# Thresholded attention and a gated mix on one core: a schedule written as a list of operations

## The chip, the cores and the metric

The kernel runs on one core of a Trainium2 chip. A core has five engines that run side by side, each with its own queue of instructions that it takes in order: PE (TensorE, matrix products and transposes), DVE (VectorE), ACT (ScalarE), POOL (GpSimd) and SP (SyncE, which here only issues transfers). An instruction waits at the head of its queue until the semaphores that it names have been reached, and all that stands behind it waits too. The metric is the device time in microseconds, the median of several executions. Before the change it is 833.94 us (three runs, 832.13 to 834.44).

## What is computed

Batch 8, 8 heads, 576 tokens, 64 channels per head. Attention keeps only scores within `tau` of the row's maximum. Its output, with the heads side by side as 512 channels, is `x` of a gated mix.

```python
scores = scale * np.matmul(q, k.transpose(0, 1, 3, 2))
thresh = np.max(scores, axis=-1, keepdims=True) - tau
scores = np.where(scores >= thresh, scores, -1000000000.0)
scores = scores - np.max(scores, axis=-1, keepdims=True)
attn = np.exp(scores)
attn = attn / (np.sum(attn, axis=-1, keepdims=True) + 1e-09)
x = np.matmul(attn, v)            # then (B, S, 512)
...
for k in range(5):                # causal convolution along the tokens
    gate_pre += conv_w[k][None, None, :] * xp[:, k:k + S, :]
gate = 1.0 / (1.0 + np.exp(-gate_pre))
out = gate * (x @ w_val) @ w_out
```

Q, K, V are float32; the weights arrive as float64 words and are converted on the chip.

## The kernel before, in words

Heads go in pairs, one over the other in the 128 partitions: 4 pairs in each of 8 batches, 32 pairs. A pair's queries make 9 tiles: one of the first 64 queries of both heads, and 4 of 128 for each head. A float32 operand of the scores and of the products with the weights is split in a high and a low part (`fp32r`), whose products are added.

For each tile: PE forms the scores in the tile `s` of PSUM, which has two rooms (`scores`, L255; four matmuls, six for the tile of both heads). DVE takes the negated maximum (L272), ACT the exponential (L274) and the threshold (L276), DVE compares, multiplies and sums up in one instruction (L292, `Group.keep`). `Group.divide` then adds 1e-9 to the sums (L301, DVE), takes the reciprocals (L304, DVE) and scales the rows (L307, POOL). `Group.turn` transposes the rows in chunks of 128 keys on PE (L319) into `tp` (two rooms of PSUM), and ACT copies them to `T` (L322).

When the tiles of half a pair's queries have been transposed (320 queries in the first half, 256 in the second), `attend_units` (L354 to L362) forms the attended values in an accumulator (`acc`, two rooms of PSUM): one matmul for the last 64 keys of both heads (L355), then eight, four chunks of keys for two heads (L362), the first head to the lower 64 columns of the array and the second to the upper 64. Each matmul of plain float32 has two records in the trace, so these are 2 and 16. The eight come in two units of four, `attend(0)` and `attend(1)`, at two steps of the loop, and within the first of them transposes may be put.

`conv_units` splits the result in two parts and convolves it: one tap on POOL (L395), four on DVE (L402), tanh on ACT (L410). `mix_units` issues the products of a batch, 192 matmuls (L429) in 16 units of 12 (320 or 256 wide), while the next batch attends. DVE multiplies by the gate (L447), ACT and POOL split the result (L452, L454), ACT takes up the second products (L467), and a transfer writes them out.

Beside all that, `Job` fetches q and k of the next pairs, splits them (L202, L204, L216, L218) and spreads the parts over the partitions with 12 transfers per pair from SP's queue (L198). The weights are converted during the first two batches, in 16 pieces of five DVE steps each (`from_f64`, L98 to L113).

The order of the work is written out by hand: the loop at L637 makes one step per tile, `stages` gives each preparation its step, `plan` and `moves` spread the products over the steps between two attentions, and `turns` holds the transposes back by two steps. On top of that the framework may still move an instruction ahead of others of its engine, since the source doesn't ask for its own order.

Of the kernel before, what the change touches and what calls it, by code (L numbers as in the profile page):

```python
# [19 lines left out]
RUN = (2, 3)  # steps between two attentions, in turn  # L20
# [3 lines left out]
def tile_thresholded_attention_gated_mix(  # L24
# [26 lines left out]
    W = [SL + 2 * P, 2 * P]  # the queries of a pair in two parts  # L51
# [9 lines left out]
    qk = ctx.enter_context(tc.tile_pool(name="qk", bufs=2))  # L61
    att = ctx.enter_context(tc.tile_pool(name="att", bufs=2))
    pt = ctx.enter_context(tc.tile_pool(name="pt", bufs=1))
    mix = ctx.enter_context(tc.tile_pool(name="mix", bufs=1))
    ps_s = ctx.enter_context(tc.tile_pool(name="ps_s", bufs=2, space=bass.MemoryType.PSUM))
    ps_t = ctx.enter_context(tc.tile_pool(name="ps_t", bufs=2, space=bass.MemoryType.PSUM))
    ps_a = ctx.enter_context(tc.tile_pool(name="ps_a", bufs=2, space=bass.MemoryType.PSUM))

# [6 lines left out]
    # a negative tau keeps no score, and all keys weigh the same: as if all scores were 0  # L75
# [8 lines left out]
    bdq = [[const.tile([P, P], F32R, name=f"bdq{i}{j}") for j in range(2)] for i in range(2)]  # L84
# [4 lines left out]
    # ---- float64 words to float32: sign, exponent and the mantissa's top 20 bits come from the  # L89
    # high word (nothing below the normal range), the next 16 from the low word's upper half ----  # L90
    def from_f64(words, a, m, f):
        """The pieces of work for a, and one that adds the low word's share."""
        i32 = lambda t: t.bitcast(I32)
        hi, lo = words[..., 1], words.bitcast(U16)[..., 1]
        least = 2.0**-15 * 1.125  # its bits are those of a high word of 2^-126

        def pieces():
            nc.scalar.square(f, hi.bitcast(F32))  # L98
            nc.vector.tensor_scalar(
                i32(m), hi, 3, 0x3FFFFFFF, op0=ALU.logical_shift_left, op1=ALU.bitwise_and  # L100
            )
            yield
            nc.vector.scalar_tensor_tensor(
                i32(a), hi, -(1 << 30), i32(m), op0=ALU.bitwise_and, op1=ALU.bitwise_or
            )
            yield
            nc.vector.scalar_tensor_tensor(
                a, f.bitcast(F32), least * least, a, op0=ALU.is_ge, op1=ALU.mult)
            yield
            nc.vector.tensor_scalar(i32(m), i32(a), -(1 << 23), None, op0=ALU.bitwise_and)  # L110
            yield
            nc.vector.scalar_tensor_tensor(f, lo, 2.0**-36, m, op0=ALU.mult, op1=ALU.mult)
            nc.gpsimd.tensor_add(a, a, f.bitcast(F32))  # L113
            yield

        return pieces()
# [5 lines left out]
    def fetch_conv():  # L122
        nc.sync.dma_start(
            cw_raw.rearrange("p (c k) t -> p c (k t)", c=NE),
            conv_w.bitcast(I32).rearrange("(c p) k -> p c k", p=P),
        )

    CW = DM // 2
    parts = [
        (name, w, c, d0)  # L130
        for name, w in (("wv", w_val), ("wo", w_out))
        for d0 in range(0, DM, CW)
        for c in range(NE)
    ]
    rooms = []
    spare = [const.tile([P, CW], F32, name=f"spare{i}") for i in range(3)]

    def fetch_mix():
        """The words of the next CW columns of 128 rows."""
        if len(rooms) < len(parts):  # L140
            _, w, c, d0 = parts[len(rooms)]
            room = mix.tile([P, S], F32, name="o", bufs=2)
            words = room[:, 0 : 2 * CW].bitcast(I32)
            nc.sync.dma_start(words, w.bitcast(I32)[c * P : (c + 1) * P, 2 * d0 : 2 * (d0 + CW)])
            rooms.append(words.rearrange("p (d t) -> p d t", t=2))

    ready = {"wv": 0, "wo": 0}  # columns

    def weights():
        """A piece of DVE's work at a time."""  # L150
        before = None
        for u, (name, _, c, d0) in enumerate(parts + [(None,) * 4]):
            if name:
                hi, lo = (t[:, c, d0 : d0 + CW] for t in w_hl[name])
                pieces = from_f64(rooms[u], spare[u % 2], spare[2], hi)
            for k in range(5):
                if name:
                    next(pieces)
                if before and k == 1:
                    nc.scalar.copy(before[1], before[0])  # L160
                if before and k == 3:
                    nc.gpsimd.tensor_sub(before[2], before[0], before[1].bitcast(F32))
                    if before[3]:
                        ready[before[3][0]] = before[3][1]
                if name or k < 3:
                    yield True
            fetch_mix()
            if name:
                before = (spare[u % 2], hi, lo, (name, d0 + CW) if c == NE - 1 else None)
            if u == 0:  # L170
                yield from from_f64(cw_raw, *cw_work)

    def spread(dst, src):
        nc.gpsimd.tensor_scalar(dst, src, 1.0, 0.0, op0=ALU.mult, op1=ALU.add)

# [1 line left out]
    class Job:  # L177
        """Pair g of batch b."""

        def __init__(self, i, b, g):  # L180
            self.i, self.b, self.g = i, b, g

        def fetch(self):
            self.k_r = raw.tile([P, SK], F32, name="k_r")
            nc.sync.dma_start(self.k_r, kT[self.b, self.g])
            self.q_r = raw.tile([P, S], F32, name="q_r")
            nc.sync.dma_start(self.q_r, qT[self.b, self.g])

        def fetch_v(self):
            self.v = qk.tile([P, (NKC + 1) * P], F32, name="v")  # L190
            nc.sync.dma_start(self.v, vs[self.b, self.g])

        def scale_q(self):
            nc.gpsimd.tensor_scalar(self.q_r, self.q_r, sc, 0.0, op0=ALU.mult, op1=ALU.add)

        def copies(self, pairs):
            for dst, src in pairs:
                nc.sync.dma_start(dst.bitcast(F32), src.bitcast(F32))  # L198

        def split_q(self, copy=True):  # L200
            qh = part.tile([P, S], F32R, name="qh")
            nc.scalar.copy(qh, self.q_r)  # L202
            ql = part.tile([P, S], F32R, name="ql")
            nc.gpsimd.tensor_sub(ql, self.q_r, qh.bitcast(F32))  # L204
            if copy:
                self.Q = qk.tile([P, 2, NKC * P], F32R, name="Q")
                for h, hs in enumerate(HEADS):
                    self.copies((self.Q[r, h, :], x[hs, SL:S]) for r, x in zip(HEADS, (qh, ql)))
            self.bd = bdq[self.i % 2]
            for dst, src in zip(self.bd, (qh, ql)):  # L210
                for hs in HEADS:
                    spread(dst[hs, hs], src[hs, 0:SL].bitcast(F32))

        def split_k(self, copy=True):
            self.kh = part.tile([P, SK], F32R, name="kh")
            nc.scalar.copy(self.kh, self.k_r)  # L216
            self.kl = part.tile([P, SK], F32R, name="kl")
            nc.gpsimd.tensor_sub(self.kl, self.k_r, self.kh.bitcast(F32))  # L218
            if copy:
                self.KH = qk.tile([P, 2, S], F32R, name="KH")  # L220
                self.KL = qk.tile([P, 2, S], F32R, name="KL")
                for dst, src in ((self.KH, self.kh), (self.KL, self.kl)):
                    for r in HEADS:
                        self.copies((dst[r, h, :], src[hs, self.window(h)]) for h, hs in enumerate(HEADS))

        def window(self, h):
            """Where the keys start: the last SL come last in the first head, first in the second."""
            return slice(SL, SK) if h == 0 else slice(0, S)

        def load_at_once(self):  # L230
# [12 lines left out]
            for h in range(2):  # L243
# [8 lines left out]
                )  # L252

# [1 line left out]
    def scores(t, h, qc):  # L255
        s = ps_s.tile([P, 2, 512], F32, name="s")
        for a in range(2):
            hs = slice(a * HS, (a + 1) * HS)
# [267 lines left out]
    def finish(tile_, weights):  # L526
        _, h, _, grp, end = tile_
        grp.keep(h or 0, *weights)
        if h == 0:
            return  # L530
# [167 lines left out]
```

## Time and profile before

| what | value |
|---|---|
| median of 3 runs | 833.94 us (832.13 to 834.44) |
| span of the profiled execution, first to last instruction | 829.6 us |
| matmul records on PE | 5216, 163 per pair |
| additive sums on DVE (L301) | 160, 58.6 us in all |
| transfers that spread the parts (L198), per pair | 12 |

The profile is that of one execution; its span leaves out what lies around the first and the last instruction. Busy time of an engine is the union of its instructions. Rows of groups read: line, engine, operation, output<-inputs, shapes, count, then the busy time in us and the mean ns of one, then the idle time of the engine just before and what ended it. Rows of the chain of waits read: start, length in us, engine, tile, line and count. The chain is followed back from the last instruction of a stretch to what released each step.

### The profile page before, as it was taken

To read this page: it belongs to the slowest core of one execution; us is meant where nothing else is said; L and a number is where in the kernel's file an instruction comes from. 1 tells how busy PE (TensorE), PEld (TensorE's weight loads), DVE (VectorE), ACT (ScalarE), POOL (GpSimd) and SP (SyncE) were. 2 spreads that over 40 slices of the span, in tenths; PEclk is the share of its full clock that TensorE was granted. 3 is DMA by queue.
4 is the path that set the end of the run, shared out by engine and by line. 5 is a ranking of instruction groups with operands and counts; after the bars stand their busy time and mean duration, and the time that the engine had idled before them with its cause. 6 is when DMAs were issued, how large, how long until landed. Compare 5 with 4: busy or idle time off the path is not lost.

```text
span 829.6 us, 15974 instructions
## 1 busy us (share of the span) xinstructions
PE 769.9 (93%) x5216; PEld 605.3 (73%) x5216; DVE 690.2 (83%) x1468; ACT 599.5 (72%) x1383; POOL 548.3 (66%) x715
## 2 busy tenths in 40 slices
PE   3878788898999999999999999999999999989998
PEld 2555455676687788777877877777778777878887
DVE  6889989999988997799888997799887997888730
ACT  5677767777777787777877877777877777867732
POOL 4687678787776766587756776677755775556421
PEclk9999999999999999999999999999999999999999
DMA  6555554544455434544554344545544445540001
GB/s 181 143 147 139 152 139 119 133 118 112 128 158 143 96 102 121 146 117 123 143 157 111 91 108 139 151 121 129 133 125 118 107 109 143 143 99 17 30 30 58
DMA packets 51890, 99.05 MB, mean 119 GB/s; under 512 B 9056, under 2 KB 9056, under 8 KB 51808
## 3 DMA queue, kind: packets, MB, share of 16 engines
q1 hardware_dynamic: 51488, 97.47, 44.3%
q8 instruction: 42, 0.69, 0.4%
q10 hardware_dynamic: 320, 0.56, 0.3%
q14 instruction: 40, 0.33, 0.1%
HBM read 35.74 MB, written 9.44 MB: 54 GB/s over the span
## 4 chain that ended last, share of the span: by engine, by line
PE 60%; DVE 28%; POOL 4%; ACT 3%; issue 2%; DMA 2%; SPq 0%; POOLq 0%; ACTq 0%; DVEq 0%
PE s L266 15%; PE acc L429 14%; PE acc L362 13%; PE tp L319 12%; DVE pre L402 8%; DVE pp L292 7%; DVE nm L272 6%; PE acc L355 3%; PE s L429 3%; DVE sums L301 3%; POOL pp L307 1%; DVE g L447 1%; DVE pl L292 1%; ACT e L274 1%; DMA pp<-qT 1%
## 5 line engine op out<-in xcount | busy, mean ns | idle before, releaser
L307 POOL TENSOR_SCALAR pp<-pp,ri 128x576 f32<-128x576 f32 x256 | 213.2, 845 | 127.7 <-DVE ri L304 98.7
L272 DVE TENSOR_REDUCE nm<-s 128x1 f32<-128x576 f32 x288 | 215.0, 748 | 56.2 <-PE s L266 55.3
L274 ACT ACTIVATE e<-s,nm 128x576 f32<-128x576 f32 x288 | 214.4, 744 | 63.3 <-DVE nm L272 38.3
L292 DVE SCALAR_TENSOR_TENSOR pp<-s,th,e 128x576 f32<-128x576 f32 x256 | 206.9, 810 | 31.0 <-ACT th L276 27.3
L322 ACT COPY T<-tp 128x384 f32<-128x384 f32 x384 | 183.4, 483 | 61.9 <-PE tp L319 59.0
L319 PE MATMUL tp<-ident,pp 128*128 128x128 f32 x1152 | 201.3, 282 | 19.3 <-POOL pp L307 16.8
L266 PE MATMUL s<-KH,Q 128*128 128x288 f32 x512 | 167.5, 342 | 28.6 <-DVE pp L292 10.9
L319 PEld LDWEIGHTS tp<-ident,pp 128*128 128x128 f32 x1152 | 137.9, 142 | 72.0 <-issue 34.5
L362 PE MATMUL acc<-T,v 128*64 128x320 f32 (+1 forms) x992 | 175.6, 420 | 0.0
L402 DVE SCALAR_TENSOR_TENSOR pre<-xT,cw,pre 128x576 f32<-128x576 f32 x128 | 145.1, 1134 | 13.2 <-POOL pre L395 13.1
L266 PE MATMUL s<-KL,Q 128*128 128x288 f32 x512 | 146.2, 300 | 0.0
L266 PEld LDWEIGHTS s<-KH,Q 128*128 128x128 f32 x512 | 100.4, 196 | 54.2 <-issue 25.7
L362 PEld LDWEIGHTS acc<-T,v 128*64 128x64 f32 x992 | 66.8, 136 | 60.4 <-issue 35.2
L266 PEld LDWEIGHTS s<-KL,Q 128*128 128x128 f32 x512 | 99.8, 195 | 0.8
L276 ACT ACTIVATE th<-nm,less 128x1 f32<-128x1 f32 x288 | 85.7, 298 | 0.6
L429 PE MATMUL acc<-xh,wvh 128*128 128x320 f32 (+1 forms) x224 | 71.4, 319 | 0.0
L429 PE MATMUL acc<-xl,wvh 128*128 128x320 f32 (+1 forms) x224 | 70.6, 315 | 0.0
L429 PE MATMUL acc<-xh,wvl 128*128 128x320 f32 (+1 forms) x224 | 67.0, 299 | 0.0
L429 PE MATMUL acc<-gh,woh 128*128 128x320 f32 (+1 forms) x212 | 66.6, 314 | 0.0
L429 PE MATMUL acc<-gl,woh 128*128 128x320 f32 (+1 forms) x212 | 66.1, 312 | 0.0
L429 PE MATMUL acc<-gh,wol 128*128 128x320 f32 (+1 forms) x212 | 63.5, 300 | 0.0
L454 POOL TENSOR_TENSOR gl<-g,gh 128x576 fp32r<-128x576 f32 x32 | 50.8, 1588 | 16.7 <-ACT gh L452 16.0
(96 smaller groups left out, 1275.2 us busy)
## 6 DMA issues: line engine op xcount, KB each, us to landing
KH<-kh SPq DMA_DIRECT2D x124, 144.0 KB, 2.5
KL<-kl SPq DMA_DIRECT2D x124, 144.0 KB, 2.6
k_r<-kT SPq DMA_DIRECT2D x32, 320.0 KB, 3.3
v<-vs SPq DMA_DIRECT2D x32, 320.0 KB, 2.9
q_r<-qT SPq DMA_DIRECT2D x32, 288.0 KB, 3.3
outT<-o SPq DMA_DIRECT2D x32, 288.0 KB, 2.1
Q<-qh SPq DMA_DIRECT2D x62, 128.0 KB, 2.3
Q<-ql SPq DMA_DIRECT2D x62, 128.0 KB, 2.3
```

What stands on the lines that cost most here:

```text
L266: nc.tensor.matmul(s[:, a, :HS], w, m, start=i == 0, stop=i == len(terms) - 1)
L272: nc.vector.tensor_reduce(nm, sv, axis=AX.XY, op=ALU.max, negate=True)
L274: nc.scalar.activation(e, sv, AF.Exp, bias=nm)
L276: nc.scalar.activation(th, nm, AF.Identity, bias=less, scale=-1.0)
L292: nc.vector.scalar_tensor_tensor(self.p[:, i * S : (i + 1) * S].rearrange("p (a f) -> p a f", a=2), sv, th, e, op0=ALU.is_ge, op1=ALU.mult ...
L307: nc.gpsimd.tensor_scalar(v, v, ri[:, i : i + 1], 0.0, op0=ALU.mult, op1=ALU.add)
L319: nc.tensor.transpose(tp[:, i * P : (i + 1) * P], self.p[:, k0 : k0 + P], ident)
L322: nc.scalar.copy(T[:, c0 : c0 + n, self.off : self.off + P], tp[:, 0 : n * P].rearrange("p (c q) -> p c q", q=P),)
L362: nc.tensor.matmul(acc[0][hs, :w], t.v[:, c0 : c0 + D], T[:, h * NKC + c, :], start=False, stop=c == NKC - 1, skip_group_check=True,)
L402: nc.vector.scalar_tensor_tensor(cv, xT[:, k : k + S], cw[:, g, k : k + 1], cv, op0=ALU.mult, op1=ALU.add)
L429: nc.tensor.matmul(ps, wt[:, c, c0 : c0 + P], m[:, hs], start=n == 0, stop=n == NM - 1)
L454: nc.gpsimd.tensor_sub(gl, g[e], gh.bitcast(F32))
```

## The change

The hand-written order goes. Every piece of work becomes an `Op` with an engine, a due time counted in tiles, a cost (how long its engine is taken, us), a time until its result is there, what it comes after, and the rooms that it takes and gives back. `carry_out` then plays the engines' time forward in the source and emits each operation when its turn comes: of the operations that could begin first on an engine, the one that is due first. The framework is asked to keep the order as it is written (`manual_schedule`). Nothing of what is computed changes.

```diff
-RUN = (2, 3)  # steps between two attentions, in turn
+PATIENCE = 0.0
+AHEAD = False
+TH = "ACT"
+DUE = (8, 8, 8)
+PACE_M = 0.17
...
+    ctx.enter_context(tc.manual_schedule())
...
+    def carry_out():
+        while True:
+            best = None
+            for e, ops in open_ops.items():
+                can = []
+                for o in ops:
+                    if all(r.free for r in o.takes):
+                        can.append((max([idle[e], o.ready] + [r.free[0][0] for r in o.takes]), o))
+                if can:
+                    first = min(t for t, _ in can) + PATIENCE
+                    t, o = min((x for x in can if x[0] <= first), key=lambda x: x[1].due)
+                    if best is None or t < best[0]:
+                        best = (t, o)
...
+            open_ops[o.engine].remove(o)
+            idle[o.engine] = t + o.cost
+            o.landed = t + o.done
+            o.emit()
...
+    r_s = Rooms(ps_s, 2, [P, 2, 512], F32, "s")
+    r_tp = Rooms(ps_t, 2, [P, 512], F32, "tp")
+    r_acc = Rooms(ps_a, 2, [P, 512], F32, "acc")
+    r_kh = Rooms(part, 1, [P, SK], F32R, "kh")
...
+    r_T = Rooms(pt, 2, [P, 2 * NKC + 1, W[0]], F32, "T")
```

The steps of a tile, with their entries (cost, then time until the result is there):

```diff
+            self.scores = op(
+                "PE", k - DUE[0], 0.80 if both else 0.54, 1.06 if both else 0.8, self.multiply,
+                after, [r_s], gives,
+            )
+            largest = op("DVE", k - DUE[1], 0.67, 0.84, self.largest, [self.scores], [r_nm])
+            if TH == "ACT":
+                after = [op("ACT", k - DUE[1], 0.83, 1.0, self.weigh, [largest], [r_e])]
...
+            grp.kept = op(
+                "DVE", k - DUE[2], 0.74, 0.96, self.keep, after, room + ([] if i else [r_sums]),
+                [(r_s, lambda: self.s), (r_e, lambda: self.e), (r_nm, lambda: self.nm)],
+            )
```

The sums' addition goes to POOL, and the reciprocals stand beside the sums in one tile:

```diff
-            nc.vector.tensor_scalar(sums, sums, 1e-9, None, op0=ALU.add)
-            ri = att.tile([P, 2], F32, name="ri", bufs=4)
-            nc.vector.reciprocal(ri[:, 0:n], sums)
+            add = op("POOL", k - 4, 0.2, 0.33, lambda: nc.gpsimd.tensor_scalar(
+                sums(), sums(), 1.0, 1e-9, op0=ALU.mult, op1=ALU.add), [self.kept])
+            inv = op("DVE", k - 4.9, 0.08, 0.33, lambda: nc.vector.reciprocal(ri(0, n), sums()), [add])
...
+                turn = op(
+                    "PE", k - 3 + 0.1 * c0, 0.109 * m, 0.109 * (m - 1) + 0.35, self.turn(c0, m),
```

The attended values of half the queries become one operation:

```diff
-                for c in (2 * part, 2 * part + 1):
+                for c in range(NKC):
                     for h, hs in enumerate(HEADS):
                         c0 = (2 * c + h) * D
                         nc.tensor.matmul(
-                            acc[0][hs, :w], t.v[:, c0 : c0 + D], T[:, h * NKC + c, :],
+                            acc[hs, :w], t.v[:, c0 : c0 + D], T[:, h * NKC + c, :],
                             start=False, stop=c == NKC - 1, skip_group_check=True,
                         )
-                    if c == 0 and sum(u[0] <= step for u in turns) > 2:
-                        mid()
-        return [attend(0), attend(1)]
+            cost = 5 * w / 600 + 0.19
+            made = op("PE", k - 2, cost, cost + 0.2, attend, [t.got_v, *self.copies], [r_acc], gives)
```

A tap of the convolution, a step of the weights, a matmul of the products, and two of the transfers from SP:

```diff
+        for i in range(1, KT):
+            last = op("DVE", k + 0.6 * i, 0.82, 0.92, tap(i), [last])
...
+        c = 0.35 if wide else 0.12
+        last = op("DVE", due, c, c + 0.1, lambda: nc.vector.tensor_scalar(
+            i32(m), hi(), 3, 0x3FFFFFFF, op0=ALU.logical_shift_left, op1=ALU.bitwise_and), after)
...
+                    cost = 0.147 if j == 0 else 0.118
+                    last = [op("PE", k, cost, cost if n < NM - 1 else 0.38, run, after,
+                               [r_acc] if n == 0 else [])]
+                    n += 1
+                    k += PACE_M
...
+                o = op("SP", due + 1, 0.15, 2.9, copies(name, rooms, src, 0), [done], [rooms])
+                o2 = op("SP", due + 1, 0.15, 2.9, copies(name, rooms, src, 1), [done, o])
```

The padding of `xT` is cleared once for its two rooms instead of once per pair, the threshold is kept beside the maximum in `nm`, and all rooms are handed out by the planner instead of the framework's pools.

More of the change, by code (lines that the diff above doesn't have):

```diff
@@ L87, in tile_thresholded_attention_gated_mix, with __init__ @@
     }
[L91 removed]
+    class Op:
+        def __init__(self, engine, due, cost, done, emit, after, takes, gives):
+            self.engine, self.due, self.cost, self.done = engine, due, cost, done
+            self.emit, self.takes, self.gives = emit, takes, list(gives)
+            self.ready = 0.0
+            self.waits = 0
+            self.next = []
+            self.landed = None
+            for a in after:
+                if a.landed is None:
+                    a.next.append(self)
+                    self.waits += 1
+                else:
+                    self.ready = max(self.ready, a.landed)
@@ new lines, in tile_thresholded_attention_gated_mix, with __init__, take, give @@
+    class Rooms:
+        def __init__(self, pool, n, shape, dtype, name):
+            self.free = [(0.0, pool.tile(shape, dtype, name=f"{name}{i}")) for i in range(n)]
+        def take(self):
+            return self.free.pop(0)[1]
+        def give(self, room, when):
+            self.free.append((when, room))
+            self.free.sort(key=lambda f: f[0])
+    open_ops = {e: [] for e in ("PE", "DVE", "ACT", "POOL", "SP")}
+    idle = {e: 0.0 for e in open_ops}
+    def op(engine, due, cost, done, emit, after=(), takes=(), gives=()):
+        o = Op(engine, due, cost, done, emit, after, takes, gives)
+        if not o.waits:
+            open_ops[engine].append(o)
+        return o
@@ new lines, in carry_out @@
+    def carry_out():
[11 more added lines that the diff above has]
+                        best = (t, o)
+            if best is None:
+                break
+            t, o = best
+            open_ops[o.engine].remove(o)
+            idle[o.engine] = t + o.cost
+            o.landed = t + o.done
+            o.emit()
+            for rooms, room in o.gives:
+                rooms.give(room(), o.landed)
+            for n in o.next:
+                n.ready = max(n.ready, idle["PE"] if o.engine == n.engine == "PE" else o.landed)
+                n.waits -= 1
+                if not n.waits:
+                    open_ops[n.engine].append(n)
+        assert not any(open_ops.values()), "some operations can never begin"
@@ L138, in fetch_mix @@
[L138 to L171, printed above, removed]
@@ new lines, in product, with run @@
+            hi, lo = w_hl[name]
+            c0 = e * P
+            n = 0
+            for c in range(NE):
+                for which, (wt, i) in enumerate(((hi, 0), (hi, 1), (lo, 0))):
+                    def run(n=n, c=c, wt=wt, i=i):
+                        if n == 0:
+                            taken[name, e, j] = r_acc.take()
+                        nc.tensor.matmul(
+                            taken[name, e, j][:, :w], wt[:, c, c0 : c0 + P], moving(c, i)[:, hs],
+                            start=n == 0, stop=n == NM - 1,
+                        )
+                    after = [need[c][i], weights[name, c, c0 // CW * CW], *last]
+                    if n == 0 and AHEAD:
+                        after += [y for x in need.values() for y in x]
+                    cost = 0.147 if j == 0 else 0.118
[3 more added lines that the diff above has]
+                    k += PACE_M
@@ L611, in tile_thresholded_attention_gated_mix @@
-    step = 0
-    converting = weights()
-    jobs[0].load_at_once()
-    jobs[0].fetch()
-    fetch_conv()
-    fetch_mix()
-    fetch_mix()
-    make_identity(nc, ident)
-    for i in range(2):
-        for t in bdq[i]:
-            nc.gpsimd.memset(t.bitcast(F32), 0.0)
-    jobs[0].scale_q()
-    s_next = scores(*tiles[0][0:3])
-    last = None
-    weights_ = None
-    def more():
-        nonlocal s_next
-        if last is not None:
-            finish(*last)
-        if step + 1 < len(tiles) and s_next is None:
-            s_next = scores(*tiles[step + 1][0:3])
-        beside()
-        while later:
-            later.pop(0)()
@@ L657 @@
+                half.copies += grp.turned(len(tiles) - 1)
+            half.attended(len(tiles) - 1)
+        convolve(t, batch, len(tiles))
+        if t.g == NP - 1:
+            last = products(batch, len(tiles) + 4.0, last)
+    carry_out()
 _INS = ["qT", "kT", "vs", "tau", "w_val", "conv_w", "w_out"]
```

829 lines of the change are left out of this document (463 added, 366 removed).

## The prediction

> **What bounds the kernel now.** I start with the page's list of busy time by engine, then cut the span into stretches, then read the chain of waits in one steady stretch, and last look at single durations.
>
> ```profile
> span 829.6 us, 15974 instructions
> PE 769.9 (93%) x5216; PEld 605.3 (73%) x5216; DVE 690.2 (83%) x1468; ACT 599.5 (72%) x1383; POOL 548.3 (66%) x715
> ```
>
> PE leads with 93%, but matmul records overlap one another, so this alone does not say that PE is full. The stretches say more (columns: length, then busy time and instruction count of PE, PEld, DVE, ACT, POOL; granted clock; DMA).
>
> ```profile
> 0.00:210.00 210.00, 166.41 (x986) 118.82 (x986) 187.99 (x409) 148.24 (x343) 154.04 (x212) 0.98 0.52 136
> 210.00:786.00 576.00, 564.98 (x3954) 452.21 (x3953) 493.83 (x1045) 438.65 (x1015) 384.93 (x496) 1.00 0.45 119
> 786.00:830.00 44.00, 38.53 (x279) 34.31 (x277) 8.36 (x16) 12.57 (x27) 9.32 (x8) 1.00 0.11 41
> ```
>
> There are three regimes. Up to 210 us (two batches, and the conversion of the weights on DVE) DVE is busy for 188 of 210 us and PE for 166. From 210 to 786 us PE is busy for 565 of 576. The last 44 us are the products of the last batch. One pair of heads has 5216/32 = 163 matmul records, so the middle stretch holds 3954/163 = 24.26 pairs at 576/24.26 = **23.74 us per pair**. The chain of waits shows whether those are dense. This is part of one pair (start, length, engine, tile, line, records):
>
> ```profile
> 404.12 0.53 PE s L266 x4
> 404.66 1.23 PE acc L362 x8
> 405.88 0.48 PE tp L319 x3
> 406.36 1.22 PE acc L362 x6
> 407.58 0.73 PE s L266 x4
> 408.32 0.68 PE acc L362 x2
> 409.00 0.48 PE tp L319 x3
> ...
> 410.59 0.33 PE tp L319 x3
> 410.92 1.18 PE acc L429 x8
> ...
> 413.75 0.95 PE acc L429 x8
> ...
> 415.66 0.43 PE acc L355 x2
> 416.09 1.01 PE acc L362 x8
> 417.11 0.26 PE tp L319
> 417.37 0.53 PE s L266 x4
> 417.90 1.01 PE acc L362 x8
> 418.92 0.48 PE tp L319 x3
> ```
>
> Every piece of the pair is PE: the middle stretch is bound by the order and the form of PE's own work, not by another engine. And the pieces are not equally dense. Three transposes take 0.33 us, but 0.48 us straight after the attended values (L362, which use half of the array's columns): leaving that form costs 0.15. The attended values of the 320 wide half come in three pieces, 8, 6 and 2 records, those of the 256 wide half in two. Six and two is no break that the source has: the framework put the scores in there, between two heads that otherwise run side by side. Near the end of the program, where little competes, the 256 wide half does run whole:
>
> ```profile
> 795.90 1.90 PE s L362 x16
> ```
>
> **The change part by part.**
>
> *Attended values in one piece.* For the 256 wide half two pieces, 1.01 + 1.01 = 2.02, become 1.90: an entry costs 0.12. For the 320 wide half I scale what is left, (1.90 - 0.12) x 320/256 + 0.12 = 2.35, against 1.23 + 1.22 + 0.68 = 3.13 now: 0.78 less, most of it because the split of 6 and 2 ran two heads one after the other. Exits go from 5 per pair to 2: 3 x 0.15 = 0.45. Together 0.12 + 0.78 + 0.45 = **1.35 us of PE per pair**, on the path: 24.26 x 1.35 = **33 us** in the middle stretch. In the first stretch I count it as nothing: there DVE hides it; were that cover gone, 8 pairs x 1.35 = 11 us more would go. The price is that PE takes no score for 2.35 + 0.54 (the two records before) = 2.9 us; that is in the rivals.
>
> *The order from the planner.* PE's work per pair without any wait is, from the rows: scores 38 x 0.53/4 = 5.04, transposes 41 x 0.33/3 = 4.51, products 24 x 1.18/8 + 24 x 0.95/8 = 6.39, the chunk of last keys 0.43 + 0.54 = 0.97, attended values 1.90 + 2.35, two exits 0.30: **21.46 us**. So of 23.74, 1.35 go with the pieces and 23.74 - 21.46 - 1.35 = 0.93 are what the present order still loses in waits and small gaps. The planner may take away all of it (24.26 x 0.93 = 23 us) or add to it; no row shows an order that has not been run. Its entries on PE fit the rows (0.54 for four score matmuls, 0.109 for a transpose, 0.147 and 0.118 for the products). On DVE it enters 0.82 for a tap of the convolution, and for the weights' steps 0.35:
>
> ```profile
> L402 DVE SCALAR_TENSOR_TENSOR pre<-xT,cw,pre x128: 790/948/2179, 52.5 to 803.3; 128x576 f32<-128x576 f32 x128
> L402 DVE SCALAR_TENSOR_TENSOR pre<-xT,cw,pre 128x576 f32<-128x576 f32 x128 | 145.1, 1134 | 13.2 <-POOL pre L395 13.1
> L99 DVE TENSOR_SCALAR spare<-o 128x256 int32<-128x256 int32 x16 | 11.3, 705 | 0.0
> ```
>
> Here 790/948/2179 are the least, median and greatest ns of a tap; the mean is 1134, so DVE runs 4 x 0.31 = 1.3 us per pair behind the plan. A step of the weights takes 705 ns, twice its entry. DVE can bear it: 493.83/24.26 = 20.36 us per pair now, 18.55 without the sums (below), 83% of 22.39. ACT has 438.65/24.26 = 18.1 (81%). I take the leftover as unchanged, **0**, with -23 us as one end and the slower rival as the other.
>
> *The sums' addition from DVE to POOL.* What DVE loses by it in each stretch, and how long one takes:
>
> ```profile
> 0.00:210.00 210.00, 14.62 (x39) 0.98 0.52 136
> 210.00:786.00 576.00, 43.81 (x120) 1.00 0.45 119
> ...
> L301 DVE TENSOR_SCALAR sums<-sums x160: 137/159/1379, 17.5 to 786.4; 128x2 f32<-128x2 f32 x128, 128x1 f32<-128x1 f32 x32
> ```
>
> In the first stretch, DVE-bound, 14.6 us of DVE go. PE, POOL and the hand-overs also set that stretch's end (DVE idles 22 of 210), so I take **10 us**; the ends are 0, and 25 if some of the idle time goes too. In the middle stretch PE hides the 43.8 us. On POOL the nearest rows are a tiny fill and a 64x64 copy:
>
> ```profile
> L371 POOL MEMSET xT<- 128x4 f32 x32 | 3.2, 101 | 18.6 <-DVE ri L304 14.3 <-DVE sums L301 2.1 <-DVE pre L402 1.6
> L174 POOL TENSOR_SCALAR bdq<-ql 64x64 fp32r<-64x64 f32 x64 | 17.1, 267 | 4.0
> L307 POOL TENSOR_SCALAR pp<-pp,ri 128x576 f32<-128x576 f32 x256 | 213.2, 845 | 127.7 <-DVE ri L304 98.7
> L454 POOL TENSOR_TENSOR gl<-g,gh 128x576 fp32r<-128x576 f32 x32 | 50.8, 1588 | 16.7 <-ACT gh L452 16.0
> ```
>
> Between 0.10 and 0.27 each, 160 of them: 16 to 43 us of POOL; I take 0.2, 32 us, in time that POOL already spends waiting (98.7 us for the reciprocals alone). POOL goes from 384.93/24.26 = 15.9 to about 16.9 us per pair, 75%. The added wait: DVE's reciprocal now waits for an addition that may stand behind a 1.59 us subtraction on POOL, and behind the reciprocal on DVE stand the next maxima and products, for which PE's next scores wait. The plan knows that hand-over, so I price it at 0; uncovered it is at most 1.6 us, five times a pair.
>
> *The remaining edits* (one memset of the padding instead of 32, threshold and reciprocal kept beside their sources, rooms taken by hand) touch no row above 0.3 us an instruction and get 0. The queue of SP keeps the same transfers; see the third rival.
>
> [...] The middle stretch has weight loads for 452.21 of 576 us, 78.5%. [...]
>
> **Sum**, against the profiled execution: 829.6 - 33 - 10 = 786.6. Between the span and the median of the three runs shown (833.94) lie 4.3 us; with them the forecast is **791 us**. The last stretch stays: it is one batch's products and hand-overs.
>
> **The rivals.**
>
> *The planner also removes the waits* (better). All 0.93 us per pair go and the first stretch loses 25: 829.6 - 24.26 x 2.28 - 25 + 4.3 = 754. For it: the planner sees all engines at once. Against it: DVE would then be 18.55 of 21.46, 86%, with rigid queues. Between 754 and 772: 0.12.
>
> [...] It needs matmuls closer together than any piece of the chain shows: 0.03.
>
> *Slower: the two rooms of scores become the bound.* Place: s has two rooms in PSUM, and each is held from PE's scores over the maximum, the exponential and the threshold to DVE's product. The plan's entries sum to 0.80 + 0.84 + 1.00 + 0.96 = 3.6 us for one life; nine tiles a pair in two rooms allow 22.39 x 2/9 = 4.98. Against the plan stand an attended piece of 2.9 us in front of a score, taps of up to 2.18 us and reciprocals waiting for POOL in front of a maximum. The order is fixed, so every queue behind stands too. The point: above 5.35 us per life a pair costs 24.1, and all of the gain (33 + 10 us, 1.77 per pair) is gone. At 5.6 us a pair takes 25.2: 791 + 24.26 x 2.8 = 859. The transfers could do the same once a pair:
>
> ```profile
> 404.05 1.76 SPq L198 DMA_DIRECT2D KH<-kh  x3
> 405.91 2.49 SPq L198 DMA_DIRECT2D KL<-kl  x4
> ```
>
> Each issue takes 0.6 us, twelve a pair, 7.2 us; the plan enters 0.15 for two. Copies that come due together land 3 us later than planned, and PE's first scores of a pair wait. Together 0.16, most of it the rooms. Against them stands what PE's scores wait for DVE's product now, with 23.74 x 2/9 = 5.28 us per life, in the middle stretch (total, times, longest):
>
> ```profile
> PE s L266 <- DVE pp L292: 0.9, 4, 0.3
> ```
>
> *Partly given back, or not done.* Waits grow by less than the gain: 810 to 831. Here too belongs that the framework goes on moving instructions, as it did with the 6 and 2: then only the first stretch gains, 829.6 - 10 + 4.3 = 824. The source now asks for the order as written, which speaks against it. 0.14. *No change*: the growth of waits happens to equal the gain, 0.03.
>
> **How the numbers follow.** Forecast (772 to 810) 0.52; better 0.12; a fifth 0.03; partly 0.14; none 0.03; slower 0.16. Within 0.3% of 833.94, about what a measurement of this kernel can tell from no change, is 831.4 to 836.4. Faster: 0.52 + 0.12 + 0.03 + 0.14 = 0.81; same 0.03; slower 0.16. The range goes from 760 (half of the better case) to 845 (the mild part of the slower one), leaving out about 0.06 + 0.03 + 0.11 = 0.20. The forecast's own range is 772 to 810.
>
> **What would show it.** Right: the attended values appear as 16 records in a row after two, with two exits per pair; a steady pair takes about 22.4 us, that is 728 matmul records per 100 us where the middle stretch has 686; DVE has no additions, and POOL has 160 short ones. DVE's share in the middle rises to some 83%. Wrong: PE's scores wait for DVE's product for more than a microsecond per tile (rooms), or for transfers once a pair (SP); the pieces are still split; or the records per 100 us stay at 686 though the pieces are whole. The forecast also fails if the first stretch grows because the weights' steps on DVE take twice what the plan enters.

## The result, and the profile after

The changed kernel takes **810.23 us** (median of four runs, 806.60 to 813.37) against 834.19 us for the kernel before in the same comparison: a ratio of 0.972, 95% interval 0.968 to 0.975. The forecast was 791, the range 760 to 845. The direction and the main cause were right, but only 24 of the 43 us came: the measured time stands at the border between the forecast's own part of the range (772 to 810) and the rival "partly given back" (810 to 831).

The page of the changed kernel, its span and its busy times, then the same three stretches as before:

```profile
span 811.6 us, 15771 instructions
PE 734.5 (91%) x5216; PEld 612.0 (75%) x5216; DVE 657.7 (81%) x1308; ACT 592.5 (73%) x1383; POOL 577.6 (71%) x843
```

```profile
0.00:210.00 210.00, 159.85 (x971) 122.64 (x972) 181.49 (x366) 144.24 (x334) 162.11 (x240) 0.92 0.54 136
210.00:786.00 576.00, 554.03 (x4096) 469.37 (x4094) 473.70 (x938) 442.99 (x1038) 410.06 (x600) 1.00 0.48 120
786.00:812.00 26.00, 20.62 (x155) 19.97 (x153) 2.54 (x6) 5.31 (x11) 5.46 (x4) 0.96 0.12 46
```

The count of PE's records (the first number in brackets) tells where the time went, since both kernels have 5216 of them. By 210 us the changed kernel has done 971 where the old one had done 986: the first stretch did not gain, it lost 15 records, some 2 us. In the middle stretch it does 4096 instead of 3954. At 576/4096 = 0.14 us each the 142 more are worth 20 us. The two together are the 18 us between the spans, 829.6 and 811.6. (The medians are 24 us apart: the profiled execution of the changed kernel, 813.37 us, was the slowest of its four, and that of the kernel before, 829.6 us of span, lies at the fast end of its scatter.) A pair in the middle takes 576 x 163/4096 = **22.92 us**: 23.74 before, 22.39 forecast. Of it PE is busy for 554.03 x 163/4096 = 22.05 us and idle for 0.87; before, it was busy for 23.29 and idle for 0.45. So the change took 1.24 us of work off PE per pair and added 0.42 us of waiting.

The chain of waits in the middle, for parts of one pair of the changed kernel (start, length, engine, tile, line, records):

```profile
402.41 0.56 PE acc L605 x2
402.98 2.30 PE acc L612 x16
405.28 0.73 PE s L467 x4
...
413.34 0.52 PE s L467 x4
413.87 0.43 PE acc L605 x2
414.30 1.88 PE acc L612 x16
416.17 0.26 PE tp L566
416.43 0.15 PE acc L703
416.58 0.55 PE s L467 x4
417.13 0.02 issue
417.15 0.76 DVE nm L471
417.91 1.84 DVE pre L661
419.75 0.03 issue
419.77 0.82 DVE pre L661
420.59 0.75 DVE pp L493 x2
421.34 0.04 issue
421.38 0.80 PE s L467 x4
```

Two things are to be seen. The attended values run whole, 16 records in 2.30 and 1.88 us (2.35 and 1.90 were worked out), and what follows pays one exit (0.73 for four score matmuls instead of 0.53). In all 64 half pairs of this trace the 16 records stand in a row on PE. And the chain leaves PE: both rooms of scores are full, and the product that would free one (L493) stands on DVE behind two taps (L661), the first of which takes 1.84 us where the plan has 0.82. What PE's matmuls waited for in the middle stretch (total us, times, longest) confirms that this is the new wait; before, the same row had 0.9 us:

```profile
PE s L467 <- DVE pp L493: 18.2, 22, 2.2
PE s L467 <- DVE pl L493: 2.4, 7, 0.4
```

Why that tap takes 1.84 us shows when POOL's row of the timeline is laid beside DVE's (start, length):

```profile
417.69 1.42 POOL L649 TENSOR_TENSOR xl<-xT,xh 128x576 fp32r<-128x576 f32 x1 [0.26 <-ACT xh L645]
417.83 1.91 DVE L661 SCALAR_TENSOR_TENSOR pre<-xT,cw,pre 128x576 f32<-128x576 f32 x1
```

POOL is subtracting at the same time. It is the rule in this trace: of the 104 taps in the middle stretch, the 16 with no POOL work beside them take 0.80 to 0.82 us, the 40 beside other work of POOL at most 1.28, and all 33 that take over 1.3 us (up to 2.13) run beside one of POOL's subtractions. DVE's products (L493), 81 of which run beside such subtractions too, stay at 0.82 or less. And the long taps are what PE waits behind: in 21 of the 22 waits above, 17.8 of the 18.2 us, a tap of more than 1.4 us is among the last four instructions that DVE runs without a break before the product.

### The profile page after: what moved, and what is told of

It reads as the page before. It is cut to its first block, busy times and chain, and to the rows that moved or that the text cites. A ratio compares the mean times of both kernels' runs of the same rounds, so it can differ in the third digit from the quotient of the medians.

```text
span 811.6 us, 15771 instructions
## 1 busy us (share of the span) xinstructions
PE 734.5 (91%) x5216; PEld 612.0 (75%) x5216; DVE 657.7 (81%) x1308; ACT 592.5 (73%) x1383; POOL 577.6 (71%) x843
## 4 chain that ended last, share of the span: by engine, by line
PE 38%; DVE 29%; POOL 16%; DMA 8%; issue 4%; ACT 2%; SPq 1%; POOLq 0%; ACTq 0%; DVEq 0%
DVE pre L661 11%; PE acc L703 11%; PE s L467 10%; PE acc L612 8%; PE tp L566 7%; DVE pp L493 7%; DVE nm L471 6%; DMA q_r<-qT 6%; POOL pp L518 5%; PE acc L605 2%; POOL ql L309 2%; POOL kl L301 2%; POOL gl L750 2%; POOL q_r L312 1%; POOL sums L510 1%
## 5 line engine op out<-in xcount | busy, mean ns | idle before, releaser
L518 POOL TENSOR_SCALAR pp<-pp,sums 128x576 f32<-128x576 f32 x256 | 209.2, 828 | 46.2 <-DVE sums L512 35.2
L493 DVE SCALAR_TENSOR_TENSOR pp<-s,nm,e 128x576 f32<-128x576 f32 x256 | 207.7, 812 | 27.7 <-ACT nm L479 25.4
L566 PE MATMUL tp<-ident,pp 128*128 128x128 f32 x1152 | 188.8, 282 | 14.6 <-POOL pp L518 8.7
L661 DVE SCALAR_TENSOR_TENSOR pre<-xT,cw,pre 128x576 f32<-128x576 f32 x128 | 150.1, 1173 | 15.2 <-POOL pre L654 14.6
L612 PE MATMUL acc<-T,v 128*64 128x256 f32 (+1 forms) x1024 | 141.6, 419 | 0.0
L510 POOL TENSOR_SCALAR sums<-sums 128x2 f32<-128x2 f32 (+1 forms) x160 | 41.1, 257 | 89.8 <-DVE pp L493 69.2
L479 ACT ACTIVATE nm<-nm,less 128x1 f32<-128x1 f32 x288 | 83.9, 291 | 0.0
L703 PE MATMUL acc<-gl,woh 128*128 128x320 f32 (+1 forms) x256 | 79.5, 311 | 1.1 <-POOL gl L750 1.1
L703 PE MATMUL acc<-gh,wol 128*128 128x320 f32 (+1 forms) x256 | 79.9, 312 | 0.0
L703 PE MATMUL acc<-gh,woh 128*128 128x320 f32 (+1 forms) x256 | 79.2, 309 | 0.4 <-ACT gh L746 0.4
L703 PE MATMUL acc<-xh,wvl 128*128 128x320 f32 (+1 forms) x256 | 78.5, 307 | 0.0
```

The source lines that it names most:

```text
L479: nc.scalar.activation(self.nm[:, 1:2], self.nm[:, 0:1], AF.Identity, bias=less, scale=-1.0)
L493: nc.vector.scalar_tensor_tensor(grp.p[:, i * S : (i + 1) * S].rearrange("p (a f) -> p a f", a=2), self.s[:, :, :HS], self.nm[:, 1:2], self.e,
L510: add = op("POOL", k - 4, 0.2, 0.33, lambda: nc.gpsimd.tensor_scalar(sums(), sums(), 1.0, 1e-9, op0=ALU.mult, op1=ALU.add), [self.kept])
L518: nc.gpsimd.tensor_scalar(v, v, ri(i), 0.0, op0=ALU.mult, op1=ALU.add)
L566: nc.tensor.transpose(tp[:, i * P : (i + 1) * P], self.p[:, k0 : k0 + P], ident)
L612: nc.tensor.matmul(acc[hs, :w], t.v[:, c0 : c0 + D], T[:, h * NKC + c, :], start=False, stop=c == NKC - 1, skip_group_check=True,)
```

## The experiments

Each kernel was timed against the kernel before. "By 210 us" is the count of PE's records until then, and the last column is the time of a pair in the stretch from 210 to 786 us, 576 x 163 over its records; both are from the profiled execution. Executions of one kernel differ by up to 8 us, and the profiled one was the slowest for changed (813.37), words_booked (818.74) and th_dve (819.18) and the fastest for two_pieces (820.51), so some dozens of records between two first stretches can be scatter (10 records are 1.4 us).

| kernel | median us | ratio to before, 95% interval | by 210 us | us per pair |
|---|---|---|---|---|
| before | 834.19 | 1 | 986 | 23.74 |
| changed | 810.23 | 0.972, 0.968 to 0.975 | 971 | 22.92 |
| two_pieces | 824.75 | 0.989, 0.986 to 0.992 | 1041 | 23.64 |
| sums_dve | 814.92 | 0.979, 0.976 to 0.982 | 992 | 23.12 |
| taps_booked | 814.33 | 0.977, 0.974 to 0.981 | 1003 | 23.19 |
| words_booked | 813.02 | 0.977, 0.972 to 0.981 | 925 | 22.88 |
| th_dve | 818.41 | 0.980, 0.976 to 0.984 | 1004 | 23.34 |
| patience | 818.34 | 0.983, 0.980 to 0.987 | 1013 | 23.33 |
| free_order | 890.64 | 1.068, 1.065 to 1.071 | 863 | 25.79 |
| old_one_piece | 856.46 | 1.027, 1.023 to 1.030 | 947 | 24.57 |
| old_sums_pool | 920.57 | 1.104, 1.099 to 1.109 | 870 | 26.93 |
| old_manual | 941.24 | 1.129, 1.126 to 1.132 | 780 | 27.21 |
| old_manual_one_piece | 1057.99 | 1.267, 1.263 to 1.272 | 670 | 30.62 |
| split_first | 804.50 | 0.965, 0.963 to 0.968 | 1019 | 22.83 |

### One part of the change undone

**two_pieces**

```diff
-            cost = 5 * w / 600 + 0.19
+            cost = 2 * w / 600 + 0.3
...
-            made = op("PE", k - 2, cost, cost + 0.2, attend, [t.got_v, *self.copies], [r_acc], gives)
+            begun = op("PE", k - 2, cost + w / 600, cost + w / 600, lambda: attend(0),
+                       [t.got_v, *self.copies], [r_acc])
+            made = op("PE", k - 2 + 0.6, cost, cost + 0.2, lambda: attend(1), [begun], [], gives)
```

> The changed kernel with the attended values of half a pair's queries as two operations of the planner (the first keys and two chunks, then two chunks) in place of one. If the whole piece is worth what the rows of the kernel before say, each half pays one entry (0.12 us) and one exit (0.15 us) more wherever PE does something else in between: up to 0.54 us per pair, 13 us over the 25 pairs of the middle stretch, so 815 to 824 us. Rival: a piece of 2.9 us that can't be interrupted starves the two rooms of scores and is what keeps the waits at 1.46 us per pair; then two shorter pieces give some of that back and the time is 800 to 808 us.

824.75 us, 14 us slower, as the whole piece's theory had it. The middle pair costs 0.72 us more: PE is busy for 551.25 x 163/3971 = 22.63 us of it, 0.58 more, close to the 0.54 expected, and the rest is waiting. PE's scores wait as long for DVE's product as with whole pieces (18.8 us, 24 times, instead of 18.2 us, 22 times), so the long piece is not what starves the rooms in the middle. But by 210 us this kernel is 70 records ahead of the changed one, which nobody expected:

```profile
0.00:210.00 210.00, 165.00 (x1041) 122.79 (x1043) 190.73 (x385) 151.81 (x355) 173.00 (x250) 0.97 0.56 143
210.00:786.00 576.00, 551.25 (x3971) 452.09 (x3968) 455.96 (x912) 438.44 (x1013) 400.06 (x587) 1.00 0.46 117
```

**sums_dve**

```diff
-            add = op("POOL", k - 4, 0.2, 0.33, lambda: nc.gpsimd.tensor_scalar(
-                sums(), sums(), 1.0, 1e-9, op0=ALU.mult, op1=ALU.add), [self.kept])
+            add = op("DVE", k - 4.9, 0.08, 0.2, lambda: nc.vector.tensor_scalar(
+                sums(), sums(), 1e-9, None, op0=ALU.add), [self.kept])
```

> The changed kernel with the sums' addition back on DVE, planned there. If moving it relieved DVE, DVE gets 160 additions of 0.14 to 1.38 us back (58.6 us in all before), the first stretch grows by up to 14.6 us and the middle one by a part of 44 us: 815 to 830 us. Rival: the hand-over from DVE to POOL and back is what DVE's reciprocals (20 us of waiting for it) and with them the scores wait for; then the time falls by up to 15 us, to 795 to 807 us.

814.92 us: the move to POOL is worth some 5 us, at the low edge of what was expected of it, and the hand-over is no net loss. The tile `sums` in this kernel (of the additions: count, then least/median/greatest ns):

```profile
L510 DVE TENSOR_SCALAR sums<-sums x160: 127/157/1517, 17.3 to 770.6; 128x2 f32<-128x2 f32 x128, 128x1 f32<-128x1 f32 x32
```

The same line in the changed kernel:

```profile
L510 POOL TENSOR_SCALAR sums<-sums x160: 191/191/821, 16.5 to 768.9; 128x2 f32<-128x2 f32 x128, 128x1 f32<-128x1 f32 x32
```

And what DVE's reciprocals wait for it there, in the middle stretch:

```profile
DVE sums L512 <- POOL sums L510: 16.6, 28, 2.1
```

On DVE an addition takes 0.16 us or up to 1.5; on POOL it takes 0.19 (median; 0.26 on average), near the 0.2 that I took, and DVE waits 16.6 us for 28 of them in the whole stretch. Of DVE's 44 us in the middle little can have been on the path. And the first stretch is not where the move pays, though that was the forecast:

```profile
0.00:210.00 210.00, 158.60 (x992) 124.43 (x993) 192.27 (x407) 145.49 (x338) 154.68 (x206) 0.93 0.55 138
```

With the additions DVE is busy for 192.27 us there instead of 181.49, and yet PE is no further behind: 992 records against 971, where 11 us would be some 75 fewer. What the move gains is in the middle, 23.12 - 22.92 = 0.20 us per pair, 5 us.

**free_order**

```diff
-    ctx.enter_context(tc.manual_schedule())
```

> The changed kernel without the request to keep the order as it is written, so that the framework may move instructions of the planner's list as it did in the kernel before. If the planner's order itself is what gained, the time goes back towards the kernel before, 820 to 834 us, and the attended values are split again. Rival: the gain is in the form of the operations (whole pieces, sums on POOL) and not in their order; then it stays at 805 to 815 us.

890.64 us, beyond both expectations: the framework's moves do not merely take the planner's gain back, they cost 80 us. The attended values mostly stay whole here (60 of the 64 pieces have their 16 records in a row; the chain has L611 with 16 in 2.30 us), so they are not the reason. The waits of this kernel are:

```profile
DVE sums L511 <- POOL sums L509: 89.1, 62, 3.7
POOL pp L517 <- DVE sums L511: 59.5, 57, 4.7
...
PE s L466 <- DVE pp L492: 45.0, 40, 4.9
```

The hand-over that costs DVE 20.2 us over the span of the planned order (33 waits) costs 89.1 over this one.

### One part done alone, in the kernel before

**old_one_piece**

```diff
-RUN = (2, 3)  # steps between two attentions, in turn
+RUN = (3, 4)  # steps between two attentions, in turn
...
-                for c in (2 * part, 2 * part + 1):
+                for c in range(NKC):
...
-        return [attend(0), attend(1)]
+        return [attend()]
```

> The kernel before with one thing changed: the attended values of half a pair's queries are issued in one step of its loop, and the steps between two attentions become 3 and 4 so that a pair still has nine. If the whole piece alone carries the gain of the middle stretch, it takes up to 1.35 us off a pair, 24 pairs: 801 to 815 us. Rival: the framework puts scores and transposes between again, or the rooms of scores starve behind 2.9 us; then 825 us or more.

856.46 us, slower by 2.7% (2.3 to 3.0). From its chain of waits, the 320 wide half:

```profile
411.32 0.79 PE acc L354 x2
...
412.43 0.68 PE acc L361 x2
...
415.20 2.30 PE acc L361 x14
```

The framework moved other work between the second and third record all the same (28 of the 64 pieces stay whole), and PE's scores wait longer (`PE s L266 <- DVE pp L292` 30.0 us in all, 12.0 before). Fewer exits alone are no gain when the steps around them are not replanned.

**old_sums_pool**

```diff
-            nc.vector.tensor_scalar(sums, sums, 1e-9, None, op0=ALU.add)
+            nc.gpsimd.tensor_scalar(sums, sums, 1.0, 1e-9, op0=ALU.mult, op1=ALU.add)
```

> The kernel before with one thing changed: the sums' addition on POOL. If DVE's relief shortens the first stretch as forecast, 10 us (0 to 15) go: 819 to 834 us, with the middle stretch as it is. Rival: in this hand-written order the addition stands on POOL behind subtractions of 1.6 us, the reciprocal on DVE waits for it and the maxima behind it: slower, 836 to 850 us.

920.57 us: the rival's mechanism, at over five times the price it was given. The waits of this kernel:

```profile
POOL sums L301 <- DVE pp L292: 122.0, 66, 4.6
...
DVE ri L304 <- POOL sums L301: 101.5, 59, 4.2
...
PE s L266 <- DVE pp L292: 68.4, 40, 4.4
```

DVE's reciprocals wait 101.5 us for POOL's additions and these 122.0 us for DVE's products, so DVE idles through the hand-over, and the products behind it are late for PE (68.4 us, 12.0 before).

**old_manual**, **old_manual_one_piece**

```diff
+    ctx.enter_context(tc.manual_schedule())
```

The second one has the edit of old_one_piece as well.

> The kernel before with one thing changed: the framework keeps the order as it is written. If the framework's moves only did harm (the split of six and two records), the middle stretch gains up to 0.5 us per pair: 820 to 830 us. Rival: the hand-written order relied on the framework to fill gaps; then it is slower, 840 us or more.

> The kernel before with both: the order kept as written, and the attended values in one piece. If whole pieces are the gain and the planner adds little, this comes near the changed kernel: 805 to 818 us. Rival: without a planner or the framework's moves the hand-written order starves PE around the long piece: 830 us or more.

941.24 and 1057.99 us: the rivals. The waits of old_manual (its lines are one higher):

```profile
ACT T L323 <- PE tp L320: 214.0, 206, 6.3
DVE nm L273 <- PE s L267: 164.0, 189, 6.6
POOL q_r L195 <- DMA q_r<-qT: 152.9, 31, 8.5
```

The hand-written list was never the order that ran. The framework's moves were worth 107 us to it, and it relied on them at almost every pair: POOL waits 31 times for a transfer of q, 152.9 us in all, where the kernel before waits 4 times, 10.7 us.

### What the leftover waits and the first stretch hang on

**taps_booked**

```diff
-            last = op("DVE", k + 0.6 * i, 0.82, 0.92, tap(i), [last])
+            last = op("DVE", k + 0.6 * i, 1.17, 1.27, tap(i), [last])
```

> The changed kernel with the convolution's taps entered in the plan at 1.17 us, the mean of their records, in place of 0.82. If the leftover waits of the middle stretch (1.46 us per pair where 0.93 was forecast) come from DVE running behind a plan that knows nothing of it, a better entry gives back a part: 798 to 806 us, a pair at 22.5 us. Rival: the waits are those of the two rooms of scores in any order at this pace; then 807 to 814 us, no change.

814.33 us, not faster; its interval overlaps that of the changed kernel. What PE's matmuls waited for in the middle stretch of this kernel:

```profile
PE s L467 <- DVE pp L493: 7.5, 12, 1.1
PE acc L703 <- POOL xl L649: 6.9, 5, 1.8
PE tp L566 <- POOL pp L518: 5.3, 11, 2.0
```

The wait for DVE's product does fall, from 18.2 to 7.5 us, so the taps ahead of it were rightly seen. But as much appears elsewhere: PE's products with the weights and its transposes now wait for POOL. The entry did not fit this order either: fewer taps ran beside a subtraction (36 of 102 in the middle stretch, 48 of 104 before), and their mean fell to 1.06 us. How long a tap takes depends on what the order puts beside it on POOL.

**th_dve**, **patience**

```diff
-TH = "ACT"
+TH = "DVE"
```

```diff
-PATIENCE = 0.0
+PATIENCE = 0.15
```

> The changed kernel with the threshold formed on DVE (288 small additions) in place of ACT, which the source offers as a setting. It takes the threshold out of the chain that holds a room of scores: exponential and threshold are 0.93 us of a life of 4.37 us in the middle stretch of the changed kernel, the exponential alone 0.75. If the leftover waits come from how long a room is held, a pair gets up to 0.8 us shorter (4.5 lives of 0.18 us): 790 to 805 us. Rival: rooms already stand empty for 0.71 us between two lives because PE comes late, so a shorter life buys nothing, and DVE has 9 x 0.15 us more per pair: 808 to 820 us.

> The changed kernel with 0.15 us of patience in the planner: an engine may stay idle that long for an operation that is due earlier. If rooms of scores stand empty because PE begins a long operation just before a score could begin, the empty time falls from 0.71 us, and the time to 798 to 806 us. Rival: idling in the plan costs what it gains; 806 to 820 us.

818.41 and 818.34 us, both slower than the changed kernel (their intervals lie wholly above 0.975, where its own ends): the rivals. In the changed kernel, over the 207 tiles whose scores begin between 222 and 745 us, a room is held for 4.37 us on average, from the first score matmul to the end of DVE's product, and then stands empty for 0.70 us until the next scores begin. In the kernel before it was 4.85 and 0.44. Neither edit did to these times what it was made for: in th_dve the room is held for 4.46 us, no shorter, and in patience it stands empty for 0.86, longer. So whether a shorter life would help was not tested. On average the rooms are not used up. They are sometimes both full while PE waits, and sometimes empty while PE does other work.

**words_booked**

```diff
-        c = 0.35 if wide else 0.12
+        c = 0.65 if wide else 0.12
```

> The changed kernel with the five steps of each piece of the weights entered at 0.65 us in place of 0.35 (705 ns was measured for one of them). If the first stretch did not get shorter because the plan takes the weights' steps for half as long as they are, the fifth pair starts up to 12 us earlier than its 120.2 us and the time falls to 798 to 804 us. Rival: the first stretch depends on chance in the plan and on PE's granted clock, which falls when PE idles there; then it may come out either way by some 8 us: 802 to 818 us, and the clock of the first 210 us moves with it.

813.02 us, no difference that the intervals show. The fifth pair begins at 115.5 us instead of 120.2, but by 210 us there are 925 records, 46 fewer, in an execution that was 6 us above this kernel's median. Longer entries for the weights' steps do not mend the first stretch.

**split_first**

```diff
-            made = op("PE", k - 2, cost, cost + 0.2, attend, [t.got_v, *self.copies], [r_acc], gives)
+            if t.b < 2:
+                cost = 2 * w / 600 + 0.3
+                begun = op("PE", k - 2, cost + w / 600, cost + w / 600, lambda: attend((0,)),
+                           [t.got_v, *self.copies], [r_acc])
+                made = op("PE", k - 2 + 0.6, cost, cost + 0.2, lambda: attend((1,)), [begun], [], gives)
+            else:
+                made = op("PE", k - 2, cost, cost + 0.2, lambda: attend((0, 1)),
+                          [t.got_v, *self.copies], [r_acc], gives)
```

> The changed kernel with the attended values in two operations in the first two batches only, where DVE sets the pace, and in one from the third batch on. The kernel with two pieces throughout had PE 1041 records on by 210 us where the changed kernel has 971, at a granted clock of 0.97 against 0.92. If the first stretch of the changed kernel is lost to the whole piece there (PE idles, its clock falls, and the piece then takes 4.29 us instead of 2.30), this kernel has both gains: 70 records more at 0.14 us, 10 us, so 797 to 804 us, with a pair of 22.9 us after the second batch. Rival: the first stretch is a matter of chance in the plan, and the plan of the middle stretch falls into another, worse pattern when the first one changes; then 806 to 820 us.

**804.50 us**, ratio 0.965 (0.963 to 0.968), just below the changed kernel's interval (0.968 to 0.975): better than both, and half a microsecond above what the first theory expected. The first stretch and the middle one of this kernel:

```profile
0.00:210.00 210.00, 162.45 (x1019) 120.10 (x1020) 187.85 (x380) 149.66 (x350) 168.12 (x247) 0.97 0.55 139
210.00:786.00 576.00, 557.75 (x4113) 472.61 (x4111) 468.83 (x929) 439.65 (x1026) 411.53 (x597) 1.00 0.47 119
```

It has 48 records more than the changed kernel by 210 us, some 7 us (the medians are 6 us apart), and keeps the middle. In the changed kernel's first stretch PE sometimes runs at a low clock, and a whole piece can meet it, as one stretch and its chain show:

```profile
90.00:100.00 10.00, 6.97 (x25) 3.31 (x24) 8.28 (x15) 4.90 (x11) 7.09 (x10) 0.66 0.85 203
```

```profile
90.49 2.12 DVE pre L661
92.61 0.75 DVE pp L493 x2
93.36 0.04 issue
93.40 1.33 PE s L467 x4
94.73 1.07 PE acc L605 x2
95.79 4.29 PE acc L612 x16
```

PE has waited 3.03 us for the product behind a long tap, it is busy for 70% of the stretch, the granted clock is 0.66, and the piece takes 4.29 us instead of 2.30, 4.29/2.30 = 1.87 times as long. In the trace of the changed kernel the granted clock is 0.50 from 92.95 to 99.78 us, and in the 3.41 us before that PE was busy for 0.55. By 210 us there are eight stretches at 0.50, and ahead of each of them PE was busy for 1.61 us or less of 3.41. But of the 14 whole pieces that begin before 210 us only two are slowed, this one and one at 32 us, by some 3 us together. Whether the clock or the order of the plan costs the rest was not separated: with the split, both changed (the granted clock of the first stretch is 0.97 instead of 0.92).

## Why the prediction was right, and where it was wrong

- **The bound.** Right. The middle stretch of the kernel before was bound by PE's own order and form; whole pieces and fewer exits shortened it. The 0.03 for "a fifth" (a fifth of the middle stretch open to a better order) rests on a term that no run shows: the lowest time of a pair in any order tried was 22.83 us (split_first), against 23.74 before, and the busy share of the weight loads rose from 78.5 to 469.37/576 = 81.5%.
- **Attended values in one piece, 1.35 us per pair.** Right in the mechanism and, within a few hundredths, in the size: 2.30 and 1.88 against 2.35 and 1.90, PE's busy time per pair fell by 1.24 us, and two_pieces, which undoes only one entry and one exit per half, gives 0.58 of it back. The rows here price the change of form at 0.12 us in, and out at 0.15 before transposes (0.48 instead of 0.33) and 0.20 before scores (0.73 instead of 0.53). Without the planner the whole piece does not pay: old_one_piece and old_manual_one_piece are both slower than the kernel before.
- **The leftover waits, taken as unchanged at 0.93 us per pair.** This step failed: they grew to 22.92 - 21.46 = 1.46, which is 25 x 0.53 = 13 us of the forecast's 33. The profile names the wait, PE's scores for DVE's product, 18.2 us instead of 0.9, and what stands ahead of the product, taps that take up to 2.1 us beside POOL's subtractions where the plan has 0.82. In its sum the prediction booked the taps only as DVE running behind the plan on average, which DVE could bear; single taps of up to 2.18 us it named in the slower rival. It is that rival's wait at a small part of its price, but not through a longer life of the rooms, which fell from 4.85 to 4.37 us. Long taps alone are not enough: in the kernel before 23 of 99 in the middle took over 1.3 us, all beside subtractions, and PE hardly waited. The order has its part: in the planner's, such taps stand in front of products that PE waits for. What removes the wait stays open: no run kept the subtractions away from the taps, and truer entries for the taps moved the waits to another place.
- **The sums' addition, 10 us in the first stretch.** This step failed too: that stretch lost 2 us. The price of one addition was about right (0.19 us in the median) and the move is worth some 5 us in all, but in the middle; in sums_dve the first stretch bears 11 us more of DVE's work and PE gets as far in it. So DVE's busy time, 188 of 210 us, does not seem to set that stretch's length, as the prediction took it to. What does is open; split_first, with two pieces there, gets some 6 us back.
- **Time around the span, 4.3 us.** Mis-sized. The profiled run of the changed kernel took 813.37 us for a span of 811.6: 1.8 us lie around it. The rest of the 4.3 was the scatter between executions. Without that scatter the gain is the 18 us of the spans, where 43 were forecast; that the median came out nearer to the forecast is luck.
- **The signs.** 163 x 100/22.92 = 711 records per 100 us came in the middle, between the 686 of before and the 728 named. DVE's share there was to rise to some 83%; it was 493.83/576 = 85.7% before, so 83% would have been a fall, and it fell to 473.70/576 = 82.2%.
- **Rivals.** That the framework would go on moving instructions did not happen, and free_order shows that it would have cost 80 us instead of leaving 824. The transfers of SP hardly stopped PE: in the page's costliest groups its scores wait 0.5 us for them. The reading of the kernel before as "written out by hand" was incomplete: its order came from the list and the framework's moves together, and old_manual prices the moves at 107 us.

## What to carry to other kernels

Count PE's records per stretch in both traces before explaining a difference of spans: here it showed at once that one stretch gained 20 us and another lost 2. An edit and its order belong together: moving 160 tiny additions to another engine cost 86 us in the old order and gained 5 in a planned one, so an edit is to be tried with the work around it replanned. Where a stage has another bound, a form that pays where PE is full (a long piece without a break) may be left out, as split_first does. A plan that gives an operation one length misses what runs beside it: the same tap took 0.8 us alone and up to 2.1 beside POOL's subtractions.

## What was not expected of the hardware

Two heads that run side by side in the two halves of the array (128*64 in the rows of the trace) did so here only where their matmuls stood next to each other: split by four score matmuls, the last two records took 0.68 us by themselves, where in a whole piece four records of both heads take 2.30/4 = 0.57. And an addition of 128x2 numbers takes 0.13 us on DVE at best and 1.52 at worst, while POOL takes 0.19 in the median (0.82 at worst). In sums_dve the 68 additions with no work of POOL beside them take at most 0.17 us on DVE, and each of the 33 that take over 0.3 ends within 0.03 us after the end of an instruction on POOL: they seem to wait for it.
